# Soft-capped attention and a squared-ReLU MLP on one core: row sums and P times V on 32-column quarters, and scores as three float32r products from batch 1 on

## The chip, the core and the metric

One core of a Trainium2 chip runs the whole kernel. The metric is device time in microseconds (us) of one execution, as the median of several runs. Before the change it is 705.87 us (three runs, 705.72 to 706.65).

## What is computed

Two stages follow one another, both in float32:

```python
def _attn_ref(q, k, v, cap):                      # q, k, v: 4 x 12 x 448 x 64
    scale = 1.0 / np.sqrt(q.shape[-1])
    scores = scale * np.matmul(q, k.transpose(0, 1, 3, 2))
    scores = cap * np.tanh(scores / cap)
    scores = scores - np.max(scores, axis=-1, keepdims=True)
    attn = np.exp(scores)
    attn = attn / (np.sum(attn, axis=-1, keepdims=True) + 1e-09)
    return np.matmul(attn, v)
...
x = attn_out.transpose(0, 2, 1, 3).reshape(B * S, H * D)   # 1792 x 768
h = x @ w_in                                      # w_in 768 x 2048
r = np.maximum(h, 0.0)
return (r * r) @ w_out                            # w_out 2048 x 768
```

## The kernel before

**Attention** works on two heads at a time (`heads`, L158): a pair, six pairs for each of the four batches, 24 in all. q and k of a pair lie transposed in one tile `qkraw`, head 0 on partitions 0 to 63 and head 1 on 64 to 127. The 448 keys are cut into four chunks of 112. For each chunk TensorE (PE in the profile) makes the transposed scores of both heads (`qk`, L186): two float32 matmuls of 64 rows, which lie on different halves of the array's rows. ScalarE (ACT) takes the tanh (L195). VectorE (DVE) keeps a running maximum over the chunks (`top`, L203), GpSimd (POOL) reduces it over the partitions (`all_top`, L211), DVE subtracts it (`less`, through the helper `sub`, L143), ACT takes the exponential (L223). A tile `t` now holds unnormalised probabilities P of one chunk, keys on partitions, queries of head 0 and then head 1 along the row.

**P times V and the row sums.** `pv` (L249) multiplies each head's 64 columns of v by its half of `t`: head 0 to output partitions 0 to 63 of the PSUM tile `po`, head 1 to 64 to 127. `ones` (L261) does the same with 64 columns of ones instead of v, so that a second PSUM tile (`ss`, which shows as `po` too) holds the sum of each query on all 64 partitions of its head. Up to pair 10 that is done for each chunk; from pair `ADD_FROM` = 11 on DVE first adds the four chunks (`add`, L233, tile `ts`) and `ones` runs once for the pair. Then ACT copies the sums (`sums`, L282), DVE transposes them in blocks of 32 (`tr1`, L285), takes 14 reciprocals on each partition (`rec`, L288), spreads them back by a second transpose (`tr2`, L291), multiplies (`mult`, L296) and splits the result into a rounded high part (`x_hi`) and a rest (`x_lo`, L143): the tile `x`, two float32r halves.

**The MLP** runs batch by batch after that batch's attention: `up` makes 16 blocks of 128 hidden units, each over six `x` tiles; `down` makes six blocks of 128 outputs, each over 16 `g` tiles. Each pair of tiles costs three float32r matmuls of 128 x 128 x 448 (L389, L390, L391: low weight by high input, high by high, high by low). That is 576 matmuls for a batch; they show as `f<-x,w` and `f<-g,w` (in the last batch `ff`).

**Weights** come in as 34 pieces: 16 of w_in (one for each block of `up`), 18 of w_out. `convert` (L315) loads a piece into `raw`, unpacks it on DVE (L339, L342, L345), splits it into high and low halves (a copy on ACT or DVE, and L143), and stores the result to device memory; batch 0 uses it from where it was made, batches 1 to 3 load it back (L378).

**What sets the order.** Nothing is scheduled by hand line by line. Each piece of work is a `Step` with an engine, a due time (`key`), a duration and buffers. At build time a planner (L475 to L569) walks through them with an event queue: each engine takes the ready step with the smallest key whose buffers fit. What comes out is one fixed order for each engine; on the chip every engine runs its list in that order and waits where data is late. The constants of L38 to L47 set the keys: `C0` is the distance of the pairs of batch 0, `W` the length planned for each batch's MLP, `EARLY` how many weight pieces are converted while batch 0's attention still runs, `SPACE` the distance of the other pieces:

```python
t0 = 2.0 + i * (TF[0] - 10.0) / EARLY if i < EARLY else TF[0] + SPACE * (i - EARLY)
to[key] = convert(t0, src, dst, n)
```

## Time and profile before

| | |
|---|---|
| median of three runs | 705.87 us (705.72 to 706.65) |
| span of the profiled execution, first to last instruction | 704.5 us |
| PE busy in the span | 688.2 us (98%), 3300 matmul instructions |
| DVE busy | 423.2 us (60%) |
| ACT busy | 362.7 us (51%) |
| POOL busy | 86.5 us (12%) |
| DMA | 148.41 MB, 211 GB/s over the span |

The span is one execution, and it ends 1.37 us below the median of the runs. Matmul times overlap in the records: a matmul's bar begins before the bar of the one ahead of it has ended, so what a matmul costs in a stream is read from start to start, not from the length of its bar. A float32 matmul stands as two instructions in the trace and as one in the printed orders below. On the other engines, too, a bar is a little longer than the distance to the next start.

### The profile page before, as it was taken

What the parts mean: (1) busy time and instruction counts of PE and PEld (TensorE: products, weight loads), DVE (VectorE), ACT (ScalarE), POOL (GpSimd) and SP (SyncE); (2) the same over time, 40 slices, a digit from 0 to 9 for tenths busy, and PEclk for the clock granted to TensorE, in tenths of its full rate; (3) what the DMA queues carried; (4) which work ended last, traced back from release to release, by engine and by line L of the source; (5) the groups of instructions that cost most, each with busy time, mean ns of one, the idle gap of its engine ahead of it and who ended that gap; (6) DMA issues with size and microseconds to landing.
All of it is one profiled execution on the core that took longest, in us unless ns stands there. A gap on an engine that the chain in (4) does not pass through costs nothing.

```text
span 704.5 us, 8604 instructions
## 1 busy us (share of the span) xinstructions
PE 688.2 (98%) x3300; PEld 500.7 (71%) x3300; DVE 423.2 (60%) x563; ACT 362.7 (51%) x498; POOL 86.5 (12%) x28
## 2 busy tenths in 40 slices
PE   6799999999999999999999999999999999999997
PEld 2233367567876786776797866766679979999997
DVE  4999999999997984777630654887681011111000
ACT  5688686788565645757521444776661003443000
POOL 1532204202101021011100110111110000000000
PEclk9899999999999999999999999999999999999999
DMA  8813469897899879745466655743337666665760
GB/s 202 262 57 107 138 219 309 273 306 259 321 324 303 300 270 333 209 149 165 153 235 206 214 182 170 227 147 127 115 116 247 239 237 214 206 209 202 241 204 26
DMA packets 57304, 148.41 MB, mean 211 GB/s; under 512 B 26288, under 2 KB 35504, under 8 KB 57264
## 3 DMA queue, kind: packets, MB, share of 16 engines
q1 hardware_dynamic: 57264, 147.87, 64.1%
q8 instruction: 26, 0.43, 0.2%
q14 instruction: 14, 0.11, 0.0%
HBM read 117.18 MB, written 30.67 MB: 210 GB/s over the span
## 4 chain that ended last, share of the span: by engine, by line
PE 87%; DVE 7%; POOL 1%; issue 1%; DMA 1%; ACT 1%; SPq 0%; ACTq 0%; DVEq 0%
PE f L389 18%; PE f L391 17%; PE f L390 17%; PE po L249 8%; PE s L186 8%; PE ff L389 5%; PE ff L390 5%; PE ff L391 5%; PE po L261 4%; DVE t L143 3%; DVE mx L203 2%; POOL ma L211 1%; DMA raw<-in_w_in_dram 1%; ACT t L223 1%; DVE xf L296 1%
## 5 line engine op out<-in xcount | busy, mean ns | idle before, releaser
L211 POOL PARTITION_ALL_REDUCE ma<-mx x24 | 86.3, 3597 | 434.0 <-DVE mx L203 412.4
L223 ACT ACTIVATE t<-t,capa 112x896 f32<-112x896 f32 x96 | 99.0, 1040 | 39.4 <-DVE t L143 38.7
L389 PE MATMUL f<-x,w 128*128 128x448 f32 x300 | 114.6, 382 | 0.0
L391 PE MATMUL f<-x,w 128*128 128x448 f32 x300 | 109.7, 366 | 0.0
L390 PE MATMUL f<-x,w 128*128 128x448 f32 x300 | 109.6, 365 | 0.0
L143 DVE TENSOR_TENSOR t<-t,ma 112x896 f32<-112x896 f32 x96 | 105.1, 1109 | 4.3 <-POOL ma L211 3.6
L389 PE MATMUL f<-g,w 128*128 128x448 f32 x288 | 106.7, 371 | 0.0
L391 PE MATMUL f<-g,w 128*128 128x448 f32 x288 | 105.3, 366 | 0.0
L390 PE MATMUL f<-g,w 128*128 128x448 f32 x288 | 105.3, 366 | 0.0
L195 ACT ACTIVATE t<-s,c 112x896 f32<-112x896 f32 x96 | 93.1, 1000 | 18.6 <-PE s L186 18.4
L186 PE MATMUL s<-qkraw 64*112 64x448 f32 x384 | 88.5, 575 | 6.4 <-DMA qkraw<-in_qkT_dram 4.7
L143 DVE TENSOR_TENSOR g<-r,g 128x448 fp32r<-128x448 f32 x64 | 40.4, 632 | 84.7 <-ACT g L138 84.6
L249 PE MATMUL po<-t,v 112*64 112x448 f32 x384 | 84.7, 553 | 4.7 <-ACT t L223 4.6
L389 PEld LDWEIGHTS f<-x,w 128*128 128x128 f32 x300 | 56.3, 188 | 35.1 <-issue 26.6
L186 PEld LDWEIGHTS s<-qkraw 64*112 64x112 f32 x384 | 31.7, 178 | 47.5 <-issue 29.8
L389 PEld LDWEIGHTS f<-g,w 128*128 128x128 f32 x288 | 54.1, 188 | 13.1 <-issue 8.9
L391 PEld LDWEIGHTS f<-x,w 128*128 128x128 f32 x300 | 56.4, 188 | 4.6
L249 PEld LDWEIGHTS po<-t,v 112*64 112x64 f32 x384 | 24.3, 137 | 49.7 <-issue 37.4
L390 PEld LDWEIGHTS f<-x,w 128*128 128x128 f32 x300 | 56.5, 188 | 3.8
L285 DVE STREAM_TRANSPOSE tr<-sm 128x448 f32<-128x448 f32 x24 | 15.4, 640 | 71.1 <-ACT sm L282 71.0
L391 PEld LDWEIGHTS f<-g,w 128*128 128x128 f32 x288 | 54.1, 188 | 4.3
L390 PEld LDWEIGHTS f<-g,w 128*128 128x128 f32 x288 | 54.2, 188 | 4.1
(52 smaller groups left out, 855.8 us busy)
## 6 DMA issues: line engine op xcount, KB each, us to landing
w<-k_in SPq DMA_DIRECT2D x48, 768.0 KB, 4.8
w<-k_out SPq DMA_DIRECT2D x36, 640.0 KB, 3.9
w<-k_out SPq DMA_DIRECT2D x18, 768.0 KB, 4.6
raw<-in_w_in_dram SPq DMA_DIRECT2D x16, 768.0 KB, 7.3
k_in<-w SPq DMA_DIRECT2D x16, 768.0 KB, 4.4
qkraw<-in_qkT_dram SPq DMA_DIRECT2D x48, 224.0 KB, 5.6
raw<-in_w_out_dram SPq DMA_DIRECT2D x12, 640.0 KB, 5.7
k_out<-w SPq DMA_DIRECT2D x12, 640.0 KB, 3.7
```

Of the source, the lines that this page charges most:

```text
L143: nc.vector.tensor_tensor(out=out, in0=in0, in1=in1, op=ALU.subtract)
L186: nc.tensor.matmul(s[c].ap[0:CP, i, 0:S], raw.ap[r, 1, ks], raw.ap[r, 0], start=True, stop=True)
L195: nc.scalar.activation(out=t[c].ap, in_=s[c].ap[0:CP, :, 0:S], func=AF.Tanh, scale=c1[0:CP])
L203: nc.vector.tensor_tensor(out=mx.ap, in0=t[0].ap if c == 1 else mx.ap, in1=t[c].ap, op=ALU.max)
L211: nc.gpsimd.partition_all_reduce(ma.ap, mx.ap, CP, RED.max)
L223: nc.scalar.activation(out=t[c].ap, in_=t[c].ap, func=AF.Exp, scale=capa[0:CP])
L249: nc.tensor.matmul(po.ap[rows[i], 0:S], vs[i].ap[:, c, rows[i]], t[c].ap[:, i], start=c == 0, stop=c == NCH - 1)
L261: nc.tensor.matmul(ss.ap[rows[i], 0:S], vs[i].ap[:, 0, rows[1 - i]], u.ap[:, i], start=start, stop=stop)
L285: nc.vector.transpose(out=tr.ap, in_=sm.ap)
L389: nc.tensor.matmul(o, w.ap[:, 1, j], x[:, 0], start=first and j == 0, stop=False)
L390: nc.tensor.matmul(o, w.ap[:, 0, j], x[:, 0], start=False, stop=False)
L391: nc.tensor.matmul(o, w.ap[:, 0, j], x[:, 1], start=False, stop=last and j == n - 1)
```

## The change

Four things change together.

1. `pv` and `ones` use quarters: four matmuls of 32 columns in place of two of 64. A quarter of `pv` is one half of a head's v columns over all 448 queries; a quarter of `ones` is one head's ones over half of the queries (224), so the tile of sums is 224 wide. `sums` and `tr1` get half as long, `rec` becomes four instructions. The rows of `x` come out in another order (32 by 32), and w_in's rows are loaded in that order, by four transfers of 32 partitions for a piece in place of one of 128.
2. From pair `SPLIT_FROM` = 6 on (batch 1 and later) q and k are split into a rounded part (`qkhi`, a copy on ACT or DVE) and a rest (`qklo`, a subtraction on DVE), and a chunk's scores are three float32r products for each head in place of one float32 product.
3. `ADD_FROM` goes from 11 to 12.
4. The planner's constants and the durations it uses for the changed steps are new; among them `EARLY` goes from 1 to 4.

```diff
@@ -32,19 +32,21 @@
     CP, NCH = v.shape[1], v.shape[3]
     NM, P, NKK, _ = w_in.shape
     NDM, _, NF, _ = w_out.shape
+    Q, SH = D // 2, S // 2
     WP = [(0, 6), (6, 5), (11, 5)]
     SCALE = 1.0 / float(D) ** 0.5
     REBASE = 2.0**-112
-    EARLY, SPACE = 1, 3.4
-    ATT, WLEAD = -6, 14
-    NBLK, NHLF, NW, XB, NT = 37, 13, 7, 10, 10
-    C0, LAT, TAIL = 4, 28, 30
-    DMA, QSTEP, HOLD, PORT = 2.5, 2, 4, 15
-    PVD, QD = 6, 2
-    XH, GH, WH = 0.0, -2.0, 0.0
-    ADD_FROM = 11
+    EARLY, SPACE = 4, 2.4
+    ATT, WLEAD = -4, 13
+    NBLK, NHLF, NW, XB, NT = 37, 13, 7, 10, 12
+    C0, LAT, TAIL = 5.0, 27, 32
+    DMA, QSTEP, HOLD, PORT = 2.5, 2, 5.0, 15.0
+    PVD, QD = 8, 2
+    XH, GH, WH = 5, -1, 4
+    ADD_FROM, SPLIT_FROM = 12, 6
+    SPLIT_DUE, NSPLIT, SPARE_H, SPARE_L, SPARE_Q = 2, 1, 2, 2, 4
     PSTEP = [2, 2, 4, 4]
-    W = [140, 145, 150, 120]
+    W = [135, 160, 160, 120]
 
     const = ctx.enter_context(tc.tile_pool(name="const", bufs=1))
     sb = ctx.enter_context(tc.tile_pool(name="sb", bufs=2))
@@ -83,7 +85,8 @@
 
     SIZES = {"blk": NBLK, "hlf": NHLF, "w": NW, "s": 2, "acc": 4, "rc": 2, "free": 1 << 20}
     TAGS = {
-        "qkraw": ("blk", [P, 2, S], F32, 3, 5),
+        "qkraw": ("blk", [P, 2, S], F32, 3, SPARE_Q),
+        "qkhi": ("blk", [P, 2, S], F32R, NSPLIT, SPARE_H), "qklo": ("blk", [P, 2, S], F32R, NSPLIT, SPARE_L),
         "s": ("s", [P, 2, 512], F32, 2, 0), "po": ("acc", [P, 512], F32, 4, 0), "f": ("acc", [P, 512], F32, 2, 0), "ff": ("acc", [P, 512], F32, 4, 0),
         "t": ("blk", [CP, 2, S], F32, NT, 2), "ts": ("blk", [CP, 2, S], F32, 2, 1),
         "mx": ("blk", [CP, 2, S], F32, 2, 2), "ma": ("blk", [CP, 2, S], F32, 2, 1),
@@ -173,6 +176,20 @@
                 nc.sync.dma_start(out=vs[i].ap[:, :, i * D:(i + 1) * D], in_=v[b, :, h + i])
 
         ready = Step(T - 16, "SP", 1.5, load, new=[raw], lag=3.0)
+        n_split = p >= SPLIT_FROM
+        operands = [raw]
+        if n_split:
+            hi, lo = Buf("qkhi"), Buf("qklo")
+            operands = [hi, lo]
+
+            def qk_hi(eng):
+                copy(eng, hi.ap, raw.ap)
+
+            def qk_lo():
+                sub(lo.ap, raw.ap, f(hi.ap))
+
+            a = Step(T - SPLIT_DUE, None, COPY(896), qk_hi, [ready], new=[hi], use=[raw])
+            ready = Step(T - SPLIT_DUE + 0.5, "DVE", SUB(896), qk_lo, [a], new=[lo], use=[raw, hi], port=True)
         got_v = Step(T, "SP", 1.4, load_v, new=vs, lag=3.0)
 
         tanhs = []
@@ -181,14 +198,17 @@
             def qk(c0=c0):
                 for c in range(c0, c0 + n_at):
                     ks = slice(c * CP, (c + 1) * CP)
-                    for i in range(2):
-                        r = slice(i * D, (i + 1) * D)
-                        nc.tensor.matmul(
-                            s[c].ap[0:CP, i, 0:S], raw.ap[r, 1, ks], raw.ap[r, 0], start=True, stop=True
-                        )
+                    pairs = [(lo, hi), (hi, hi), (hi, lo)] if n_split else [(raw, raw)]
+                    for n, (kk, qq) in enumerate(pairs):
+                        for i in range(2):
+                            r = slice(i * D, (i + 1) * D)
+                            nc.tensor.matmul(
+                                s[c].ap[0:CP, i, 0:S], kk.ap[r, 1, ks], qq.ap[r, 0],
+                                start=n == 0, stop=n == len(pairs) - 1,
+                            )
 
             cs = slice(c0, c0 + n_at)
-            q = Step(T + (2 if b == 0 else QD) * c0, "PE", 0.75 * n_at, qk, [ready], new=s[cs] + t[cs], use=[raw], mode="rows")
+            q = Step(T + (2 if b == 0 else QD) * c0, "PE", (0.57 if n_split else 0.75) * n_at, qk, [ready], new=s[cs] + t[cs], use=operands, mode="rows")
             for c in range(c0, c0 + n_at):
 
                 def tanh(c=c):
@@ -240,14 +260,16 @@
                 ]
 
 
-        rows = [slice(0, D), slice(D, 2 * D)]
+
+        quarters = [(i, a, slice((2 * a + i) * Q, (2 * a + i + 1) * Q)) for a in range(2) for i in range(2)]
 
         def pv(c0, n):
             def go():
                 for c in range(c0, c0 + n):
-                    for i in range(2):
+                    for i, a, to in quarters:
+                        d0 = i * D + a * Q
                         nc.tensor.matmul(
-                            po.ap[rows[i], 0:S], vs[i].ap[:, c, rows[i]], t[c].ap[:, i], start=c == 0, stop=c == NCH - 1
+                            po.ap[to, 0:S], vs[i].ap[:, c, d0:d0 + Q], t[c].ap[:, i], start=c == 0, stop=c == NCH - 1
                         )
                     if not n_add:
                         ones(t[c], c == 0, c == NCH - 1)
@@ -257,9 +279,11 @@
             return go
 
         def ones(u, start, stop):
-            for i in range(2):
+
+            for i, a, to in quarters:
+                d0 = (1 - i) * D
                 nc.tensor.matmul(
-                    ss.ap[rows[i], 0:S], vs[i].ap[:, 0, rows[1 - i]], u.ap[:, i], start=start, stop=stop
+                    ss.ap[to, 0:SH], vs[i].ap[:, 0, d0:d0 + Q], u.ap[:, i, a * SH:(a + 1) * SH], start=start, stop=stop
                 )
 
         n_pv = PSTEP[b]
@@ -269,7 +293,7 @@
             end = c1_ == NCH
             pvs.append(
                 Step(
-                    T + 17 + 2 * (c1_ - 1) + (PVD if b else 0), "PE", (0.75 if n_add else 1.5) * n_pv + (0.75 if n_add and end else 0),
+                    T + 17 + 2 * (c1_ - 1) + (PVD if b else 0), "PE", (0.75 if n_add else 1.125) * n_pv + (0.375 if n_add and end else 0),
                     pv(c0, n_pv), exps[c0:c1_] + [got_v] + pvs[-1:] + adds * end,
                     new=[po, ss] if c0 == 0 else [],
                     use=t[c0:c1_] + vs + ([po, ss] if c0 else []) + ([ts] if n_add and end else []), mode="cols",
@@ -279,13 +303,18 @@
         sm, tr, rc, xf, x = Buf("sm"), Buf("tr"), Buf("rc"), Buf("xf"), Buf("x")
 
         def sums():
-            nc.scalar.activation(out=sm.ap, in_=ss.ap[:, 0:S], func=AF.Identity, bias=eps)
+            nc.scalar.activation(out=sm.ap[:, 0:SH], in_=ss.ap[:, 0:SH], func=AF.Identity, bias=eps)
 
         def tr1():
-            nc.vector.transpose(out=tr.ap, in_=sm.ap)
+            nc.vector.transpose(out=tr.ap[:, 0:SH], in_=sm.ap[:, 0:SH])
 
         def rec():
-            nc.vector.reciprocal(out=rc.ap, in_=tr.ap.rearrange("p (j c) -> p j c", c=32)[:, :, 0])
+            for a in range(2):
+                own = tr.ap[a * D:(a + 1) * D, 0:SH].rearrange("p (j c) -> p j c", c=32)[:, :, 0]
+                for to in range(2):
+                    nc.vector.reciprocal(
+                        out=rc.ap[to * D:(to + 1) * D, a * SH // 32:(a + 1) * SH // 32], in_=own
+                    )
 
         def tr2():
             nc.vector.transpose(
@@ -302,9 +331,9 @@
             sub(x.ap[:, 1], xf.ap, f(x.ap)[:, 0])
 
         T += 26
-        a = Step(T, "ACT", 0.63, sums, pvs[-1:], new=[sm], use=[ss])
-        a = Step(T + 1, "DVE", 0.57, tr1, [a], new=[tr], use=[sm])
-        a = Step(T + 1, "DVE", 0.17, rec, [a], new=[rc], use=[tr])
+        a = Step(T, "ACT", 0.42, sums, pvs[-1:], new=[sm], use=[ss])
+        a = Step(T + 1, "DVE", 0.33, tr1, [a], new=[tr], use=[sm])
+        a = Step(T + 1, "DVE", 0.6, rec, [a], new=[rc], use=[tr])
         a = Step(T + 1, "DVE", 0.56, tr2, [a], use=[rc, sm])
         a = Step(T + 1, "DVE", 0.54, mult, [a] + pvs[-1:], new=[xf], use=[sm, po])
         a = Step(T + 2, None, COPY(448, dve=XH), x_hi, [a], new=[x], use=[xf])
@@ -312,13 +341,19 @@
         x_t[b, h // 2], xdone[b, h // 2] = x, a
 
 
-    def convert(T, src, dst, n):
+    def convert(T, src, dst, n, by_quarters):
         raw, u, mag, w = Buf("raw", [P, n * P]), Buf("u", [P, n * P]), Buf("mag", [P, n * P]), Buf("w", [P, 2, n, P])
         flat = lambda: u.ap.bitcast(F32)
         part = lambda i: w.ap[:, i].rearrange("p n c -> p (n c)")
 
         def load():
-            nc.sync.dma_start(out=raw.ap, in_=src.rearrange("p n c -> p (n c)"))
+            if not by_quarters:
+                nc.sync.dma_start(out=raw.ap, in_=src.rearrange("p n c -> p (n c)"))
+                return
+            rows = src.rearrange("(i a r) n c -> i a r (n c)", i=2, a=2)
+            for i in range(2):
+                for a in range(2):
+                    nc.sync.dma_start(out=raw.ap[(2 * a + i) * Q:(2 * a + i + 1) * Q], in_=rows[i, a])
 
         def word(i):
             return raw.ap.bitcast(U32).rearrange("p (n t) -> p n t", t=2)[:, :, i]
@@ -459,7 +494,7 @@
     ]
     for i, (to, key, src, dst, n) in enumerate(pieces):
         t0 = 2.0 + i * (TF[0] - 10.0) / EARLY if i < EARLY else TF[0] + SPACE * (i - EARLY)
-        to[key] = convert(t0, src, dst, n)
+        to[key] = convert(t0, src, dst, n, to is conv_in)
     for b in range(B):
         t0, rate = TF[b], W[b] / (NM * NKK + NDM * NF)
         for m in range(NM):
```

**Where the order moves.** VectorE, between the end of the fifth and of the sixth `x` tile (the last of batch 0; `x<-xf,x` is `x_lo`). Before:

```order
L143 TENSOR_TENSOR x<-xf,x 128x448
L342 TENSOR_SCALAR u<-raw 128x768
L285 STREAM_TRANSPOSE tr<-sm 128x448
L143 TENSOR_TENSOR t<-t,ma 112x896
L288 RECIPROCAL rc<-tr 128x14
L143 TENSOR_TENSOR t<-t,ma 112x896
L291 STREAM_TRANSPOSE sm<-rc 128x448
L345 SCALAR_TENSOR_TENSOR u<-mag,u 128x768
L296 TENSOR_TENSOR xf<-po,sm 128x448
L140 CAST w<-u 128x768
L143 TENSOR_TENSOR t<-t,ma 112x896
L143 TENSOR_TENSOR x<-xf,x 128x448
```

In the change:

```order
L374 TENSOR_SCALAR u<-raw 128x768
L146 TENSOR_TENSOR qklo<-qkraw,qkhi 128x896
L377 TENSOR_SCALAR u<-raw 128x768
L380 SCALAR_TENSOR_TENSOR u<-mag,u 128x768
L309 STREAM_TRANSPOSE tr<-sm 128x224
L315 RECIPROCAL rc<-tr 64x7 x4
L146 TENSOR_TENSOR t<-t,ma 112x896
L320 STREAM_TRANSPOSE sm<-rc 128x448
L146 TENSOR_TENSOR w<-u,w 128x768
L325 TENSOR_TENSOR xf<-po,sm 128x448
L146 TENSOR_TENSOR t<-t,ma 112x896
L146 TENSOR_TENSOR x<-xf,x 128x448
```

A whole weight piece (both L374/L377 halves, L380 and the `w` subtraction) and a `qklo` subtraction stand ahead of that tile now, the transposed sums are 224 wide, and the reciprocal is four instructions. Over the whole list up to the sixth `x` tile, six weight pieces are done in the change, and three before (with a fourth unpacked), and two `qklo` subtractions are new.

TensorE, the last chunk of the fourth pair and what follows it. `v_2` and `v_3` are the tiles that hold v and the ones of the two heads. Before:

```order
L249 MATMUL po<-t,v_2_110 64x448
L249 MATMUL po<-t,v_3_112 64x448
L261 MATMUL po<-t,v_2_110 64x448
L261 MATMUL po<-t,v_3_112 64x448
L389 MATMUL f<-x,w 128x448
L390 MATMUL f<-x,w 128x448
L391 MATMUL f<-x,w 128x448
L186 MATMUL s<-qkraw 112x448 x4
```

In the change:

```order
L271 MATMUL po<-t,v_2_110 32x448
L271 MATMUL po<-t,v_3_112 32x448
L271 MATMUL po<-t,v_2_110 32x448
L271 MATMUL po<-t,v_3_112 32x448
L285 MATMUL po<-t,v_2_110 32x224
L285 MATMUL po<-t,v_3_112 32x224
L285 MATMUL po<-t,v_2_110 32x224
L285 MATMUL po<-t,v_3_112 32x224
L205 MATMUL s<-qkhi,qklo 112x448 x2
L205 MATMUL s<-qkhi 112x448 x2
L205 MATMUL s<-qklo,qkhi 112x448 x2
```

A chunk has eight quarters where it had four halves, the ones' quarters 224 wide; the float32 scores (`qkraw`, two chunks in the one row before) have become three float32r products for a chunk.

SyncE, which issues the transfers, where the conversion of w_in is under way. Before:

```order
L321 DMA raw<-in_w_in_dram 128x768
L356 DMA k_in_69<-w 128x1536
L321 DMA raw<-in_w_in_dram 128x768 x2
L356 DMA k_in_70<-w 128x1536
L356 DMA k_in_71<-w 128x1536
L321 DMA raw<-in_w_in_dram 128x768
L173 DMA v_0_106<-in_v_dram 112x4x64
L173 DMA v_1_108<-in_v_dram 112x4x64
L356 DMA k_in_72<-w 128x1536
L321 DMA raw<-in_w_in_dram 128x768
```

In the change:

```order
L356 DMA raw<-in_w_in_dram 32x768 x4
L172 DMA qkraw<-in_qkT_dram 64x2x448 x2
L356 DMA raw<-in_w_in_dram 32x768 x8
L391 DMA k_in_72<-w 128x1536
L176 DMA v_0_106<-in_v_dram 112x4x64
L176 DMA v_1_108<-in_v_dram 112x4x64
L356 DMA raw<-in_w_in_dram 32x768 x8
L391 DMA k_in_73<-w 128x1536
L391 DMA k_in_74<-w 128x1536
L356 DMA raw<-in_w_in_dram 32x768 x8
```

Each piece of w_in is four rows' worth of issues, and two pieces are asked for together.

## Rows read from the trace of the kernel before

**Rows 1.** The page, busy tenths of DVE in 40 slices of the span.

```profile
DVE  4999999999997984777630654887681011111000
```

**Rows 2.** Windows: length, busy us (instructions) of PE, PEld, DVE, ACT, POOL; clock, DMA share, GB/s.

```profile
0.00:93.78 93.78, 81.03 (x359) 29.62 (x359) 84.08 (x105) 67.94 (x78) 28.42 (x11) 0.96 0.52 145
93.78:259.98 166.20, 166.20 (x801) 118.94 (x800) 158.77 (x226) 113.61 (x158) 24.89 (x6) 1.00 0.88 302
259.98:704.50 444.52, 440.94 (x2145) 352.18 (x2143) 180.32 (x234) 181.16 (x264) 33.21 (x11) 1.00 0.58 191
```

**Rows 3.** Timeline of PE, four places: start, us, engine, line, matmul.

```profile
93.78 0.47 PE L389 MATMUL f<-x,w 128*128 128x448 f32 x1
...
259.98 0.36 PE L389 MATMUL f<-x,w 128*128 128x448 f32 x1
...
584.03 0.36 PE L389 MATMUL f<-g,w 128*128 128x448 f32 x1
...
700.56 0.36 PE L391 MATMUL ff<-g,w 128*128 128x448 f32 x1
```

**Rows 4.** Timeline of PE, a step of scores, and one of P times V.

```profile
95.19 1.76 PE L186 MATMUL s<-qkraw 64*112 64x448 f32 x8
...
104.07 0.37 PE L391 MATMUL f<-x,w 128*128 128x448 f32 x1
104.37 0.97 PE L249 MATMUL po<-t,v 112*64 112x448 f32 x4
...
107.84 0.36 PE L390 MATMUL f<-x,w 128*128 128x448 f32 x1
```

**Rows 5.** Timeline of weight loads in the same P times V step.

```profile
104.37 0.20 PEld L249 LDWEIGHTS po<-t,v 112*64 112x64 f32 x4 [0.31 <-issue]
104.80 0.14 PEld L261 LDWEIGHTS po<-t,v 112*64 112x64 f32 x2 [0.23 <-issue]
```

**Rows 6.** The page, groups of weight loads: busy us and mean ns of one.

```profile
L186 PEld LDWEIGHTS s<-qkraw 64*112 64x112 f32 x384 | 31.7, 178 | 47.5 <-issue 29.8
...
L249 PEld LDWEIGHTS po<-t,v 112*64 112x64 f32 x384 | 24.3, 137 | 49.7 <-issue 37.4
```

**Rows 7.** Timeline of DVE around the sixth x tile.

```profile
86.71 0.62 DVE L285 STREAM_TRANSPOSE tr<-sm 128x448 f32<-128x448 f32 x1
...
88.23 0.22 DVE L288 RECIPROCAL rc<-tr 128x14 f32<-128x14 f32 x1
88.37 1.02 DVE L143 TENSOR_TENSOR t<-t,ma 112x896 f32<-112x896 f32 x1
...
89.87 0.91 DVE L345 SCALAR_TENSOR_TENSOR u<-mag,u 128x768 uint32<-128x768 uint32 x1
90.71 0.61 DVE L296 TENSOR_TENSOR xf<-po,sm 128x448 f32<-128x448 f32 x1
91.24 0.54 DVE L140 CAST w<-u 128x768 fp32r<-128x768 f32 x1
91.70 1.08 DVE L143 TENSOR_TENSOR t<-t,ma 112x896 f32<-112x896 f32 x1
92.71 0.61 DVE L143 TENSOR_TENSOR x<-xf,x 128x448 fp32r<-128x448 f32 x1
93.24 0.95 DVE L143 TENSOR_TENSOR w<-u,w 128x768 fp32r<-128x768 f32 x1
94.11 1.08 DVE L143 TENSOR_TENSOR t<-t,ma 112x896 f32<-112x896 f32 x1
95.11 1.08 DVE L339 TENSOR_SCALAR u<-raw 128x768 uint16<-128x768 uint16 x2
```

**Rows 8.** Tile raw: landing; timelines of SP and DVE: a load's issue, its first use.

```profile
DMA to landing us min/median/max: 4.9/6.3/10.3
...
110.34 0.42 SPq L321 DMA_DIRECT2D raw<-in_w_in_dram  x1
...
120.55 0.62 DVE L339 TENSOR_SCALAR u<-raw 128x768 uint16<-128x768 uint16 x1
```

## The prediction

> **What bounds the kernel now.** I read the slices of the page first, then the windows, then the timelines of PE and DVE. The slices show DVE full from the second slice to the thirteenth, 18 to 229 us [rows 1], and far from it behind that, so the 60% of the table is an average over very different stages. The windows put the first border at 93.78 us: before it PE is busy for 81 of 94 us, with overlapping bars, behind it without a gap [rows 2]. That is the start of the first MLP matmul that reads the sixth `x` tile [rows 3], which DVE finishes just before: its last part starts at 92.71 [rows 7]. From there on PE has no gap: 166.20 busy of 166.20 us up to 259.98, where the first matmul of batch 1's MLP stands, and all of the rest but the tail [rows 2, 3]. DVE is still busy for 158.77 of those 166.20 us (96%), and for 180.32 of the last 444.52 [rows 2]. So there are three stages: up to 93.78 DVE, with PE waiting; up to 259.98 PE, with DVE close behind; then PE alone. PE's clock is 1.00, its upper level of 2.4 GHz, in the last two.
>
> **Prices on PE, start to start.** The 576 matmuls of the last MLP have nothing among them: 584.03 to 700.56 is 575 intervals [rows 3], 0.2027 us each. A step of two chunks of P times V with ones (8 float32 rounds, two heads side by side) lies between two MLP matmuls at 104.07 and 107.84 [rows 4]: 3.77 us. I take a float32 round of 448 columns as 0.75 us for a chunk's pair, so 3.00 for the step; less two MLP matmuls (0.41) that leaves 0.36 for going in and out of the mode, 0.18 a change; I use 0.19. A score step of two chunks has a bar of 1.76 [rows 4], which agrees with 0.75 a chunk.
>
> These prices must give the time before. In the order before, from 93.78 on, stand 2274 MLP matmuls (460.9), 66 score chunks (49.5), 70 chunks of P times V (52.5), 31 of ones (23.25) and 109 changes of mode (20.7): 606.9 us. 93.78 + 606.9 = 700.7, and the last matmul starts at 700.56 and takes 0.20. The sum closes, so nothing else is on PE's path.
>
> **PE's part of the change.** In the new order the same point (the first MLP matmul that reads the sixth `x` tile, the 31st in both) is followed by 2274 MLP matmuls, 64 score chunks, all as three products, 72 chunks of P times V, 36 of ones, 105 changes.
> - Ones: a quarter has half the columns, so 0.375 a chunk if four quarters run side by side as two halves do: 36 x 0.375 = 13.5 in place of 23.25, though there are more of them (one pair fewer is added on DVE).
> - P times V: quarters of 448 columns, 0.75 a chunk as before if four run side by side: 54.0.
> - Scores: three rounds of one float32r product, two heads side by side. The trace has no such product on 64 rows; the nearest is the 128-row one at 0.2027. I take 0.608 a chunk: 38.9. The lower bound is the float32 price over four passes, 0.1875 a round (0.56 a chunk, 2.9 less in all), the upper 0.75 a chunk (9 more).
> - Changes: 20.0.
>
> With 460.9 that is 587.3, or 19.6 less than 606.9.
>
> Two prices above rest on four quarters side by side, which the trace of before does not show. What it shows is two halves side by side: four weight loads begin within 0.06 us of each other (0.20 for four bars of 0.137), and the next two begin at 104.80, while matmuls run [rows 5, 6]. A load takes 178 ns for 112 columns and 137 for 64 [rows 6], so I estimate 0.11 for 32. Four of them, 0.02 apart, take 0.17 a round: hidden under a round of 0.375, and only just under the ones' round of 0.19. The lower bound for a chunk of ones is 0.375, the upper 0.75 (no gain).
>
> The Trainium skill speaks against this, in "TensorE: Matmul & The Clock Gate", Part 3: loads of weights overlap running matmuls only where the row group differs, and quarters that share their 112 rows do not differ in it. Here the trace disagrees: the two halves share their rows too, and the loads at 104.80 begin beside running matmuls. By that rule each quarter round would show its 0.17 us of loads, and the sum would be that of the third rival below.
>
> **DVE's part, up to the sixth x tile.** PE starts its gapless run when DVE has made that tile, so every microsecond that DVE's list grows ahead of it moves the run. Counted in the two orders up to there, priced start to start [rows 7]: four more unpacking halves (0.50 each, 2.0), two more L380 (0.84, 1.7), three more `w` subtractions (0.87, 2.6), two `w` copies fewer (0.46, -0.9), two `qklo` subtractions (priced as a `t` one, 1.01: 2.0) and one `t` subtraction fewer (-1.0); six transposes of half the width (0.62 now; I estimate 0.25 off each, -1.5); 24 reciprocals in place of six (0.14 each, 2.5). Sum: **7.4 us**. The small reciprocals are the unknown: between a quarter of 0.14 each, as a quarter of the work (5 in place of 7.4), and the whole bar of 0.22 (9.3). I stay with 0.14: a transpose of 448 columns has a bar of 0.62, so little of a 14-column instruction's 0.14 can go with its length.
>
> So the tile's last part starts at 92.71 + 7.4 = 100.1, ends 0.53 later, and PE's run starts near 100.8 in place of 93.78. PE has less to do before (ones and scores are cheaper there too) and simply waits more: what the change saves in this stage buys nothing.
>
> **After that, up to the end of batch 0's MLP.** PE: 546 MLP matmuls (110.7), 20 score chunks (12.2), 24 of P times V (18.0), 24 of ones (9.0), 42 changes (8.0): 157.9 in place of 166.2. That puts the start of batch 1's MLP at 258.7, against 259.98 now. DVE has 158.77 us in this stage now; the pieces done earlier leave it, and five more `qklo` and a `qkhi` copy come in: to the last weight piece the two lists add up alike (within 1 us), so it has some 152 us in 158. It stays just ahead. What hides it is thin, and I come back to it. The work on ACT (some `qkhi` copies at about 1 us, shorter `sums`) lies in a stage with 113.61 busy of 166.20 [rows 2].
>
> Then PE alone: 587.3 - 157.9 = 429.4 in place of 606.9 - 166.2 = 440.7, so 11.3 us less. The other eleven `qklo`, the `qkhi` copies and the small reciprocals on DVE, some 25 us, lie in 444 us of which it uses 180: hidden.
>
> **w_in in four transfers.** An issue holds SP for about 0.4 us [rows 8], so the last quarter of a piece is asked for 1.2 us later. A load lands 6.3 us after its issue (median), and the piece asked for at 110.34 is first touched at 120.55 [rows 8], so 4 us are spare: nothing, if four transfers of 32 partitions together move like one of 128. If they went one after the other, each as long as the whole, it would be 25 us a piece.
>
> **Sum.** 100.8 + 587.3 = 688.1 for the last matmul; the tail to the end of the span is 704.5 - 700.8 = 3.7; span 691.8. The median of the runs lies 1.4 above the profiled span: **693.2 us**, 12.7 faster. Own range 686 to 700: scores -2.9 to +3 (half way to the upper bound), reciprocals -2.4 to +2, ones up to +4.5 if a round takes a quarter longer than its columns.
>
> **Rivals.**
> 1. Quarters run two at a time. Then a round of four costs double: after the start of the run 54.0 + 13.5 = 67.5 us more, 761. For it: no row shows more than two side by side. Against: the loads of the next round stand beside the present one without loss. This is the one that ends slower, and it decides early: the gain of 12.7 is gone once quarter rounds take 19% longer than I price them.
> 2. DVE or the loads fall behind between 100 and 259. The lists are nearly equal there (DVE 96% busy [rows 2]), DMA is at 0.88, and a quartered load that lands 4 us late holds DVE, then PE, one for one. Price 5 to 15 us: 698 to 708.
> 3. The quarters' loads are not hidden: 216 rounds x 0.17 = 37 us, 730. If only the ones' short rounds suffer, up to no gain from them: 13.5, 707. For it: 0.17 under 0.19 is close. Against: loads beside running matmuls [rows 5].
> 4. DVE's additions ahead of the sixth tile cost nothing, because it now waits in places that they fill: 686. Against: the slices show no such holes [rows 1].
>
> **Chances.** Forecast 0.58, rival 1 0.06, rival 2 0.13, rival 3 0.13 (0.05 in full, 0.08 for ones only), rival 4 0.10. A measurement tells 0.2%, 1.4 us, from no change. Faster: forecast, rival 4, most of rival 2: 0.79. Same: 0.06, from the ones-only case and the end of rival 2. Slower: 0.15. The range 684 to 707 leaves out rivals 1 and 3 in full, a little of rival 2, and the best of rival 4: about 0.18.
>
> **What would show it.** Right: PE's gapless run starts at 99 to 102 and the 577th MLP matmul at 257 to 261; eight quarters of P times V and eight of ones take 2 x 1.125 us for two chunks; scores 1.2 us for two chunks. Wrong: steps of P times V that are longer than before, gaps of PE between 100 and 259 that end with `w` or `raw`, or a run that starts as early as before.

## The result, and the profile after

The changed kernel takes **697.44 us** (median of four runs, 696.38 to 698.09), beside 705.88 us (705.72 to 706.65) for the kernel before on the same chip: a ratio of 0.9874, with an interval of 0.9861 to 0.9888. The forecast was 693.2 us, with a range of 684 to 707. The profiled execution took 698.09 us, its span is 696.3.

**The three stages** stand in the windows (length, busy us of PE, PEld, DVE, ACT, POOL; clock, DMA share, GB/s) and in the timeline of PE at their borders; they answer to [rows 2] and [rows 3]. L424 to L426 are now the lines of the MLP matmuls, L205 the scores, L271 P times V, L285 the ones, L146 the helper `sub`.

```profile
0.00:101.29 101.29, 73.26 (x559) 29.04 (x559) 91.72 (x129) 71.28 (x83) 29.96 (x11) 0.93 0.58 156
101.29:262.09 160.80, 160.73 (x1050) 123.05 (x1051) 154.82 (x233) 114.04 (x162) 30.95 (x6) 0.98 0.91 292
262.09:696.30 434.21, 430.30 (x2473) 357.90 (x2471) 206.23 (x298) 181.21 (x264) 33.87 (x11) 1.00 0.63 197
```

```profile
98.16 0.45 PE L205 MATMUL s<-qkhi,qklo 64*112 64x448 f32 x2 [1.22 <-ACT t L215]
...
101.29 0.74 PE L424 MATMUL f<-x,w 128*128 128x448 f32 x1 [2.27 <-ACT x L141]
...
262.09 0.37 PE L424 MATMUL f<-x,w 128*128 128x448 f32 x1
...
692.02 0.37 PE L426 MATMUL ff<-g,w 128*128 128x448 f32 x1
```

PE's gapless run starts at 101.29 in place of 93.78 and batch 1's MLP at 262.09 in place of 259.98. The change is 2.1 us late there, and makes all of its gain in the stage in which PE is alone: from 262.09 to the end of the last matmul are 430.1 us, against 440.8. The middle stage has no gap, but its clock is 0.98.

**What released the run** differs between the two kernels. Before, PE's last wait was for `xf` (the product that the sixth tile is made from) at 91.37; from there to 93.78 it worked through P times V and ones, and the first matmul on the sixth tile waited for nothing. In the change nothing stands in between: DVE makes `xf`, ACT rounds it, and PE starts. Timelines of PE before, then of DVE and ACT in the change:

```profile
91.37 0.97 PE L261 MATMUL po<-t,v 112*64 112x448 f32 x4 [0.52 <-DVE xf L296]
```

```profile
99.95 0.61 DVE L325 TENSOR_TENSOR xf<-po,sm 128x448 f32<-128x448 f32 x1
100.66 0.58 ACT L141 ACTIVATE x<-xf 128x448 fp32r<-128x448 f32 x1 [0.94 <-DVE xf L325]
```

**The quarters** run four side by side. Two chunks of P times V and ones between two MLP matmuls, in PE's timeline:

```profile
114.96 0.37 PE L426 MATMUL f<-x,w 128*128 128x448 f32 x1
115.26 0.96 PE L271 MATMUL po<-t,v 112*32 112x448 f32 x8
116.03 0.56 PE L285 MATMUL po<-t,v 112*32 112x224 f32 x8
116.41 0.94 PE L271 MATMUL po<-t,v 112*32 112x448 f32 x8
117.16 0.56 PE L285 MATMUL po<-t,v 112*32 112x224 f32 x8
117.66 0.47 PE L424 MATMUL f<-x,w 128*128 128x448 f32 x1
117.97 0.36 PE L425 MATMUL f<-x,w 128*128 128x448 f32 x1
```

From 114.96 to 117.97 are 3.01 us: two MLP matmuls (0.41), two changes of mode (from 128-row matmuls to quarters and back), and the quarters. With 0.18 for a change, as before, the quarters take 2.25, which is 2 x (0.75 + 0.375). The timeline of weight loads answers to [rows 5]:

```profile
115.26 0.16 PEld L271 LDWEIGHTS po<-t,v 112*32 112x32 f32 x8 [0.31 <-issue]
115.66 0.13 PEld L285 LDWEIGHTS po<-t,v 112*32 112x32 f32 x4 [0.25 <-issue]
```

Eight loads with a mean of 112 ns (the page's group) lie in one bar of 0.16, and the next four begin at 115.66, while the matmuls of 115.26 run. The Trainium skill, in "TensorE: Matmul & The Clock Gate", Part 3, lists that loads overlap running matmuls only where the row group differs, while its text above the list also excepts loads to the background weight buffer. By the list alone a load's time would stand between the rounds; the trace disagrees, as it did for the halves. Which buffer a load goes to, no run here shows.

**The scores** of two chunks, PE's timeline again:

```profile
147.05 0.37 PE L426 MATMUL f<-x,w 128*128 128x448 f32 x1
147.34 0.46 PE L205 MATMUL s<-qkhi,qklo 64*112 64x448 f32 x2
147.64 0.37 PE L205 MATMUL s<-qkhi 64*112 64x448 f32 x2
...
149.05 0.37 PE L425 MATMUL f<-x,w 128*128 128x448 f32 x1
```

147.05 to 149.05 is 2.00 us: 0.41 for two MLP matmuls, 0.38 for two changes, and 1.21 for six rounds, 0.202 each and 0.606 a chunk, as priced (0.608).

**DVE ahead of the sixth `x` tile**, its timeline beside [rows 7]:

```profile
94.06 2.28 DVE L380 SCALAR_TENSOR_TENSOR u<-mag,u 128x768 uint32<-128x768 uint32 x1
96.26 0.40 DVE L309 STREAM_TRANSPOSE tr<-sm 128x224 f32<-128x224 f32 x1
96.69 0.82 DVE L315 RECIPROCAL rc<-tr 64x7 f32<-64x7 f32 x4
97.55 1.09 DVE L146 TENSOR_TENSOR t<-t,ma 112x896 f32<-112x896 f32 x1
...
101.48 0.62 DVE L146 TENSOR_TENSOR x<-xf,x 128x448 fp32r<-128x448 f32 x1
```

Four reciprocals of 64x7 take 0.86 from start to start, 0.21 each, and not 0.14. The tile's last part starts at 101.48, forecast 100.1. L380 takes 2.28 here, and about 0.9 elsewhere; the last section comes back to that.

**The clock** in windows of 2 us around the start of the run (same columns as above; the last three numbers begin with the clock):

```profile
96.00:98.00 2.00, 0.94 (x7) 0.45 (x6) 1.90 (x7) 1.63 (x2) 0.71 (x1) 1.00 0.00 0
98.00:100.00 2.00, 0.85 (x6) 0.45 (x6) 2.00 (x4) 1.16 (x2) 0.00 (x0) 1.00 0.00 0
100.00:102.00 2.00, 0.71 (x2) 0.50 (x2) 2.00 (x4) 1.34 (x2) 0.00 (x0) 0.51 0.63 246
102.00:104.00 2.00, 2.00 (x10) 1.22 (x12) 2.00 (x3) 2.00 (x4) 0.00 (x0) 0.50 0.93 234
...
106.00:108.00 2.00, 2.00 (x25) 0.68 (x17) 2.00 (x3) 2.00 (x5) 0.00 (x0) 0.78 0.99 215
108.00:110.00 2.00, 2.00 (x11) 1.86 (x11) 2.00 (x4) 0.89 (x2) 0.36 (x1) 1.00 1.12 256
```

PE is busy for under half of 96 to 102, with waits of 1.22 and 2.27 us for ACT, and then starts its run at 1.2 GHz. From 101.29 to 106 at half the clock it loses 2.35 us of work, from 106 to 108 at 0.78 another 0.44: 2.8 in all. The forecast for this stage was 157.9 us, and it took 160.80. The size of the loss differs from one execution to the next: a second profile of the same kernel (the run "changed kernel once more" below) has the stage from 101.36 to 260.83, 159.47 us.

### The profile page after: what moved, and what is told of

Its sections match the earlier page's. It is cut to its first block, busy times and chain, and to the rows that moved or that the text cites. A ratio compares the mean times of both kernels' runs of the same rounds, so it can differ in the third digit from the quotient of the medians.

```text
span 696.3 us, 10384 instructions
## 1 busy us (share of the span) xinstructions
PE 664.3 (95%) x4080; PEld 510.0 (73%) x4080; DVE 452.8 (65%) x658; ACT 366.5 (53%) x508; POOL 94.8 (14%) x28
## 4 chain that ended last, share of the span: by engine, by line
PE 86%; DVE 9%; issue 2%; DMA 1%; ACT 1%; SPq 1%; DVEq 0%; ACTq 0%
PE f L424 18%; PE f L426 17%; PE f L425 17%; PE po L271 8%; PE s L205 8%; PE ff L426 5%; PE ff L424 5%; PE ff L425 5%; DVE t L146 3%; PE po L285 2%; DVE mx L223 1%; DVE u L380 1%; DMA raw<-in_w_in_dram 1%; DVE w L146 1%; DVE rc L315 1%
## 5 line engine op out<-in xcount | busy, mean ns | idle before, releaser
L231 POOL PARTITION_ALL_REDUCE ma<-mx x24 | 94.6, 3945 | 452.2 <-DVE mx L223 360.8
L424 PE MATMUL f<-x,w 128*128 128x448 f32 x300 | 114.9, 383 | 2.9 <-ACT x L141 2.3
L426 PE MATMUL f<-x,w 128*128 128x448 f32 x300 | 110.6, 369 | 1.0 <-DVE x L146 0.9
L146 DVE TENSOR_TENSOR t<-t,ma 112x896 f32<-112x896 f32 x96 | 107.2, 1132 | 5.0 <-POOL ma L231 4.6
L424 PE MATMUL f<-g,w 128*128 128x448 f32 x288 | 107.0, 371 | 0.0
L426 PE MATMUL f<-g,w 128*128 128x448 f32 x288 | 105.3, 365 | 0.0
L271 PE MATMUL po<-t,v 112*32 112x448 f32 x768 | 87.3, 561 | 8.6 <-ACT t L243 7.9
L223 DVE TENSOR_TENSOR mx<-mx,t 112x896 f32<-112x896 f32 x48 | 51.9, 1082 | 58.0 <-ACT t L215 57.2
L146 DVE TENSOR_TENSOR g<-r,g 128x448 fp32r<-128x448 f32 x64 | 40.9, 643 | 72.7 <-ACT g L141 72.5
L424 PEld LDWEIGHTS f<-x,w 128*128 128x128 f32 x300 | 56.6, 189 | 22.3 <-issue 11.8
L426 PEld LDWEIGHTS f<-x,w 128*128 128x128 f32 x300 | 56.6, 189 | 7.3 <-DVE x L146 2.5
L424 PEld LDWEIGHTS f<-g,w 128*128 128x128 f32 x288 | 54.1, 188 | 9.7 <-issue 5.1
L426 PEld LDWEIGHTS f<-g,w 128*128 128x128 f32 x288 | 54.1, 188 | 4.4
L271 PEld LDWEIGHTS po<-t,v 112*32 112x32 f32 x768 | 21.6, 112 | 43.5 <-issue 27.8
L442 ACT ACTIVATE r<-f 128x448 f32<-128x448 f32 x50 | 27.0, 542 | 43.3 <-PE f L426 42.9
L471 ACT ACTIVATE o<-f 128x448 f32<-128x448 f32 x18 | 9.7, 542 | 73.6 <-PE f L426 73.6
```

Source lines behind the costliest of these rows:

```text
L146: nc.vector.tensor_tensor(out=out, in0=in0, in1=in1, op=ALU.subtract)
L223: nc.vector.tensor_tensor(out=mx.ap, in0=t[0].ap if c == 1 else mx.ap, in1=t[c].ap, op=ALU.max)
L231: nc.gpsimd.partition_all_reduce(ma.ap, mx.ap, CP, RED.max)
L271: nc.tensor.matmul(po.ap[to, 0:S], vs[i].ap[:, c, d0:d0 + Q], t[c].ap[:, i], start=c == 0, stop=c == NCH - 1)
L424: nc.tensor.matmul(o, w.ap[:, 1, j], x[:, 0], start=first and j == 0, stop=False)
L426: nc.tensor.matmul(o, w.ap[:, 0, j], x[:, 1], start=False, stop=last and j == n - 1)
```

## The experiments

Two theories stood against each other for the 4.2 us by which the forecast was too low: that PE's clock fell around the long wait (**the clock**), and that DVE or the loads were slightly late in the middle stage (**lateness**). Beside them, several prices of the forecast were put to a run. Times stand as medians and as ratios to the kernel before in the same series (706.27 to 706.66 us).

**Halves instead of quarters.** The order of the work is kept; P times V and the ones go back to halves, the reciprocals to one instruction, a `w_in` piece to one transfer.

```diff
-                    for i, a, to in quarters:
+                    for i in range(2):
...
-            nc.vector.transpose(out=tr.ap[:, 0:SH], in_=sm.ap[:, 0:SH])
+            nc.vector.transpose(out=tr.ap, in_=sm.ap)
...
+            nc.vector.reciprocal(out=rc.ap, in_=tr.ap.rearrange("p (j c) -> p j c", c=32)[:, :, 0])
...
-            if not by_quarters:
+            if True:
```

> The changed kernel in its own order on every engine, but P times V and the row sums on 64-column halves again (sums 448 wide, one reciprocal, w_in in one transfer). My theory: behind the first MLP matmul that reads the sixth x tile stand 36 chunks of ones, 0.375 us dearer each: +13.5. Ahead of it DVE has 18 reciprocals fewer (24 x 0.20 against 6 x 0.14: -4.0) and six wider transposes (+1.5), so the run starts 2.5 earlier; the loss by the slower clock behind the wait (2.8) may go with it. 697.4 + 13.5 - 2.5 = 708.4, or 705.6 if the clock stays up. Rival, that the new order and not the quarters brings the gain: 697 to 698.

It took 713.32 us, ratio 1.0100 (1.0083 to 1.0116): slower than the kernel before, where 705.6 to 708.4 was expected. From the start of batch 1's MLP on, the ones cost what they should: 262.09 to 692.02 is 429.93 in the changed kernel, 271.29 to 705.75 is 434.46 here, and the 4.5 more are 12 x 0.375. The rest was lost earlier. Its last matmul, and two of its windows:

```profile
705.75 0.37 PE L420 MATMUL ff<-g,w 128*128 128x448 f32 x1
```

```profile
0.00:102.89 102.89, 82.59 (x366) 30.54 (x366) 88.56 (x111) 72.06 (x83) 29.47 (x11) 0.93 0.55 153
102.89:271.29 168.40, 167.26 (x858) 123.53 (x859) 150.71 (x216) 114.12 (x163) 27.38 (x6) 1.00 0.82 281
```

DVE has 18 instructions fewer ahead of the run, and still the run starts at 102.89, 1.6 us later. The view of DVE's waits up to there (total us, times, longest) says why:

```profile
DVE x L146 <- ACT x L141: 3.0, 2, 2.3
DVE tr L308 <- ACT sm L305: 2.4, 3, 1.0
```

Neither row is there for the changed kernel up to 101, where the waits of DVE on work of other engines are 6.5 us at the start and then one of 0.2. PE's longer steps of ones (82.59 us busy against 73.26) make the scores and the sums late; ACT waits for them (2.05 us for scores at 53.85, for one), and DVE behind it. PE's saving ahead of the run was not idle after all.

**One float32 product of the rounded parts.** The splitting stays, but scores are one float32 product: their rests are left out.

```diff
-                    pairs = [(lo, hi), (hi, hi), (hi, lo)] if n_split else [(raw, raw)]
+                    pairs = [(hi, hi)] if n_split else [(raw, raw)]
...
-                                s[c].ap[0:CP, i, 0:S], kk.ap[r, 1, ks], qq.ap[r, 0],
+                                s[c].ap[0:CP, i, 0:S], f(kk.ap)[r, 1, ks], f(qq.ap)[r, 0],
```

`f(...)` hands the rounded part over as float32.

> The changed kernel in its own order, the split of q and k still done on DVE and ACT, but each chunk's scores as one float32 product of the rounded parts (the rests are left out of the scores). My theory: 64 chunks on PE's gapless path at 0.75 in place of 0.608: +9.1, so 706.5; the eight chunks ahead of the run are hidden. Rival, that the three products save nothing where they stand: 697.4.

706.21 us, ratio 0.9997 (0.9988 to 1.0006), as expected. From the start of batch 1's MLP to the last matmul it takes 435.94 us, 6.0 more than the changed kernel; the 44 chunks there at 0.142 each give 6.2.

```profile
263.77 0.36 PE L424 MATMUL f<-x,w 128*128 128x448 f32 x1
...
699.71 0.37 PE L426 MATMUL ff<-g,w 128*128 128x448 f32 x1
```

**Twelve MLP matmuls moved into the hole.** Four sets of three, on `x` tiles 4 and 5 of the first two units, go to just ahead of the first matmuls on the sixth tile.

```diff
...
+            prev[0].place = (b, m, j)
...
+    late = [st for st in ISSUE if getattr(st, "place", None) in [(0, 0, 3), (0, 0, 4), (0, 1, 3), (0, 1, 4)]]
+    ISSUE[:] = [st for st in ISSUE if st not in late]
+    at = next(i for i, st in enumerate(ISSUE) if getattr(st, "place", None) == (0, 0, 5))
+    ISSUE[at:at] = late
```

> The changed kernel with four groups of MLP matmuls (12 matmuls, hidden units 0 and 1 by x tiles four and five) moved on PE from earlier to right before the first matmul that reads the sixth x tile, where PE waits 2.27 us; all other engines keep their order. My theory, that the clock fell to 0.5 behind that wait and cost 2.8 us of the stretch to batch 1: granted clock 1.00 from 100 us on, the run starts at 101.3 to 101.8, batch 1's first MLP matmul at 259 to 260, time 694.8. Rival, that the stretch is longer because weights or DVE are late: 697.4, the same 262 for batch 1.

696.62 us, ratio 0.9859 (0.9845 to 0.9874), 1.8 above what was expected. Taking the matmuls from where they stood left a hole there: PE is busy for 1.82 of 94 to 98, and the clock is 0.63 from 98 to 102. The clock had been expected at 1.00 from 100 us on; it fell earlier, and is back at 1.00 from 102. So the run starts at 102.18, but the stage behind it takes 157.82 us (102.18 to 260.00).

**The same matmuls redone.** Nothing moves; ahead of the sixth tile the first unit's 15 matmuls on tiles 1 to 5 run once more into the same sums, started anew.

```diff
+                if again and j == 5:
+                    for jj in range(5):
+                        x = rhs[jj].ap
+                        nc.tensor.matmul(o, w.ap[:, 1, jj], x[:, 0], start=jj == 0, stop=False)
+                        nc.tensor.matmul(o, w.ap[:, 0, jj], x[:, 0], start=False, stop=False)
+                        nc.tensor.matmul(o, w.ap[:, 0, jj], x[:, 1], start=False, stop=False)
...
```

> The changed kernel, but before the first MLP matmul that reads the sixth x tile PE computes hidden unit 0's first five products once more (15 matmuls, 3.0 us of work that brings nothing, in the 2.27 us wait). By the clock theory: the run starts 0.8 later and the clock stays at 1.00, so 697.4 + 0.8 - 2.8 = 695.4, faster although there is more to do. Rival, that the clock isn't what it lost: 697.4 + 0.8 = 698.2.

695.93 us, ratio 0.9849 (0.9835 to 0.9864), which overlaps with the interval of the changed kernel; what counts here is the trace. The windows of 98 to 102 and of the stage, and its one wait in PE's timeline:

```profile
98.00:102.00 4.00, 4.00 (x21) 3.61 (x20) 4.00 (x6) 3.06 (x4) 0.00 (x0) 1.00 0.56 172
...
101.25:260.42 159.17, 157.67 (x1051) 122.06 (x1050) 152.19 (x232) 112.98 (x161) 27.32 (x6) 1.00 0.92 294
```

```profile
184.35 0.47 PE L431 MATMUL f<-g,w 128*128 128x448 f32 x1 [1.50 <-DVE w L146]
```

With PE kept busy the clock stays at 1.00 and the stage's work takes 157.67 us. But now DVE is late once, by 1.50 us: lateness appears when the loss by the clock is gone.

**One transfer per `w_in` piece.** The host hands `w_in` over with its rows in the new order.

```diff
-            if not by_quarters:
+            if True:
...
-        "w_in": moe_w_in.view(np.int64).reshape(DM // P, P, DFF // P, P).transpose(2, 1, 0, 3),
+        "w_in": moe_w_in.view(np.int64).reshape(DM // P, 2, 2, 32, DFF // P, P).transpose(0, 2, 1, 3, 4, 5).reshape(DM // P, P, DFF // P, P).transpose(2, 1, 0, 3),
```

> The changed kernel in its own order, but w_in's rows are laid out in the order of the quarters in device memory beforehand, so that a piece of w_in is one transfer of 128 partitions again (16 issues in place of 64). My theory, that four transfers cost nothing: the same within a measurement, 697.4 (696.4 to 698.4), the same 160.8 us from the start of the run to batch 1. Rival, that late quarters of w_in hold DVE in the first 150 us: up to 3 us less, and the start of the run earlier.

698.24 us, ratio 0.9892 (0.9875 to 0.9908), the stage from 101.55 to 261.15: nothing is gained. The page lists the issues of w_in's pieces with their size and the median us from issue to landing, with four transfers and then with one:

```profile
raw<-in_w_in_dram SPq DMA_DIRECT2D x64, 192.0 KB, 5.3
```

```profile
raw<-in_w_in_dram SPq DMA_DIRECT2D x16, 768.0 KB, 6.2
```

A quarter lands 5.3 us after its own issue, the whole piece 6.2 after its. So the four quarters move side by side; the 25 us of the prediction's "one after the other" do not arise.

**A weight piece later.** The unpacking of the sixth piece (six steps with its store) moves behind the sixth `x` tile on every engine.

```diff
...
+        made.append(steps[-6:])
...
+    late = [st for st in ISSUE if st in made[5]]
+    last_x = xdone[0, H // 2 - 1]
+    early = [st for st in late if ISSUE.index(st) < ISSUE.index(last_x)]
+    ISSUE[:] = [st for st in ISSUE if st not in early]
+    at = ISSUE.index(last_x) + 1
+    ISSUE[at:at] = early
```

> The changed kernel with the unpacking of the sixth weight piece (two halves, the whole, its copy, its rest and its store; 2.8 us of DVE) moved from before to right after the last part of the sixth x tile; PE keeps its order. My theory, that each microsecond of DVE's list ahead of that tile moves the start of PE's run: the start at 98.3 to 99.3 in place of 101.3, no wait for x, clock 1.00 behind it. But DVE's list up to the last piece stays as long, so PE runs into waits for w of 1 to 2 us between 100 and 200, and batch 1 starts at 258.5 to 260: 694 to 695.5, the gain being mostly the clock's. Rival, that something else (PE, ACT) sets the start: 101, and 697.4.

697.86 us, ratio 0.9882 (0.9867 to 0.9896): nothing gained, against 694 to 695.5. PE's timeline:

```profile
98.91 0.47 PE L427 MATMUL f<-x,w 128*128 128x448 f32 x1 [1.23 <-ACT x L141]
...
104.47 0.58 PE L272 MATMUL po<-t,v 112*32 112x448 f32 x4 [0.76 <-ACT t L244]
...
127.51 0.47 PE L427 MATMUL f<-x,w 128*128 128x448 f32 x1 [1.72 <-DVE w L146]
```

The run starts 2.4 us earlier, as it should, and batch 1 at 262.06, where it stood (262.09). Two things were expected otherwise: a wait of 1.23 for `x` is left ahead of the run, and the clock is 0.91 from 100 to 120, not 1.00. The stage takes 163.15 us in place of 160.80: 2.48 are the two waits in it. What is taken from DVE's list ahead of the run is owed right behind it.

**The new code under the old planner's constants**, `ADD_FROM` = 11 among them.

```diff
-    EARLY, SPACE = 4, 2.4
-    ATT, WLEAD = -4, 13
+    EARLY, SPACE = 1, 3.4
+    ATT, WLEAD = -6, 14
...
-    XH, GH, WH = 5, -1, 4
-    ADD_FROM, SPLIT_FROM = 12, 6
+    XH, GH, WH = 0.0, -2.0, 0.0
+    ADD_FROM, SPLIT_FROM = 11, 6
...
-    W = [135, 160, 160, 120]
+    W = [140, 145, 150, 120]
```

> All of the change's code (quarters, four transfers, split scores), but the planner's constants of the kernel before (and its due times and lead values), which gives another order on every engine. Adding up its lists at the same prices: the sixth x tile 3.6 us later than in the change, batch 1 about 6 us later, the end 4.5 later. My theory: 699 to 703. Rival, that the gain is the retuned order's: 705 or more; rival, that the constants do nothing: 697.

715.54 us, ratio **1.0131** (1.0112 to 1.0149): slower than before, far off the 699 to 703. PE's timeline, and two windows:

```profile
67.89 0.60 PE L285 MATMUL po<-t,v 112*32 112x224 f32 x4 [5.04 <-DVE xf L325]
...
85.17 0.60 PE L285 MATMUL po<-t,v 112*32 112x224 f32 x4 [5.19 <-DVE xf L325]
...
108.79 0.60 PE L285 MATMUL po<-t,v 112*32 112x224 f32 x4 [3.06 <-DVE xf L325]
```

```profile
80.00:100.00 20.00, 13.32 (x117) 5.80 (x121) 17.44 (x28) 8.86 (x11) 3.49 (x2) 0.83 0.36 114
100.00:120.00 20.00, 16.27 (x115) 10.03 (x107) 12.83 (x21) 11.04 (x15) 2.17 (x1) 0.83 0.43 114
```

PE waits for DVE's `xf`, which frees its PSUM tile, and DVE itself is idle for 2.6 and 7.2 us of these windows. The first matmul on the sixth tile starts at 111.94, 10.7 us later than in the changed kernel, where 3.6 was expected. Engines that wait for one another in turn are in no sum of lists. All of the loss lies ahead of batch 1's MLP: from its first matmul (279.15) to the last one (710.19) are 431.0 us, nearly the 429.9 of the changed kernel. So the cheaper matmuls give the gain behind batch 1 in either order, and the order decides whether it is lost ahead of it. The rival of the expectation, that the gain is the new order's, has its time (705 or more), but the order by itself is not enough: with halves in the new order the kernel is slower than before.

**Three more in one series.** The changed kernel once more; all `w_hi` copies on ACT, to take load off DVE; and that together with the redone matmuls.

```diff
+    for st in ISSUE:
+        if st.fn.__name__ == "w_hi":
+            st.eng = "ACT"
```

> The changed kernel unaltered, as the measure of the two runs beside it: 0.987 of the time before, 697 us, the start of PE's run at 101 to 102, the clock at 0.83 to 0.91 in the stretch from 100 to 120.

> The changed kernel with all copies of the weights' rounded half on ACT (the seven that DVE does go to ACT, none of them ahead of the sixth x tile), nothing else moved. It takes 2.3 us off DVE's list between the sixth x tile and the twentieth weight piece. My theory: the start (101.3) and the fall of the clock stay, no wait for w was there to remove: 696.4 to 697.4. Rival, that DVE's list sets the time of the whole stretch to batch 1: 2 to 3 less, 695.

> Both: the 15 repeated matmuls that keep PE at work through the wait for the sixth x tile, and the weight copies on ACT. My theory: the clock stays at 1.00 behind the start (worth 2.8), and the 1.5 us wait for w that the first of these met at 184 us is gone, so batch 1 starts at 258.5 to 259.5 and the time is 694 to 694.8, the best of all. Rival, that another wait takes its place: 695.6, as with the repeat alone.

In that order: 696.34 us, ratio 0.9863 (0.9849 to 0.9877); 697.48, 0.9870 (0.9856 to 0.9883); 695.84, 0.9850 (0.9837 to 0.9864). The changed kernel came out as expected (start at 101.36, clock 0.91 from 100 to 120). The copies alone change nothing that can be told from it, though the run starts at 102.36 and not, as expected, at 101.3. Both together give the stage as it was forecast, in the windows:

```profile
101.69:259.37 157.68, 157.68 (x1051) 122.19 (x1050) 149.33 (x224) 117.64 (x168) 32.10 (x6) 1.00 0.92 297
```

No wait, clock 1.00, 157.68 us. It has the shortest median of the series, but its interval overlaps with that of the changed kernel: it cannot be called faster than that one.

## Why the prediction was right, and where not

The forecast held in kind and in size (12.7 us faster, 8.4 measured), by its own mechanism: a later start of the run, paid back by cheaper work on PE.

- **Prices on PE: right.** Ones at 0.375, P times V at 0.75, scores at 0.608 a chunk and 0.19 a change give 429.4 us from the start of batch 1's MLP on; 430.1 were measured. The runs with halves (4.5 us for 12 chunks) and with one float32 product (6.0 for 44) confirm two of them singly.
- **DVE's list ahead of the sixth tile: 7.4 us, 8.8 measured** (92.71 to 101.48). The mis-sized term is the reciprocals: 24 times 0.07 more than 0.14 is 1.7. Summed start to start over both timelines of DVE, the reciprocals grow by 4.1 (forecast 2.5) and all else by 4.7 (forecast 4.9); in the latter, single terms are off by up to 1.9, both ways, since other instructions are the slow ones beside GpSimd (last section).
- **The start of the run: 100.8, and 101.29 measured, in part by luck.** The prediction lets the run follow the tile's last part by 0.7 us. But before, the first matmul on the tile waited for no part of it (91.37, above); in the change it waits for the rounded part from ACT, and starts 0.2 ahead of the last part. `xf` moved by 9.2 us, the run by 7.5. The list was 1.4 too short and the distance 0.9 too long, and that leaves 0.5.
- **The stage up to batch 1: 157.9, and 160.80 measured.** This is the mis-sized term that counts. The step that failed is that PE "simply waits more" ahead of the run, as if that had no price behind it: with PE waiting, the clock fell to 1.2 GHz, and the run began with 2.8 us lost (1.8 in the second profile, 159.47 less 157.67). That the clock is the cause is shown by three runs: where PE was kept busy (157.67 of work, and 157.68) and where the clock had fallen and risen earlier (157.82) the stage took what was forecast. In the changed kernel itself lateness has nothing to explain: the stage has 0.07 us of gaps.
- **"What the change saves in this stage buys nothing": wrong.** With halves the run starts 1.6 us later although DVE's list is shorter. I estimate what the cheaper ones ahead of the run were worth at some 4 us: the 1.6, and the 2.5 by which the start was expected earlier.
- **Counting lists: a lower bound that the new order happens to reach.** The prediction gave the new constants no term of their own. The same code under the old constants takes about 18 us more (715.54 against 697.44). The prediction came near the time because DVE's list in the new order is nearly free of waits; the prediction did not work that out, so it is luck too. The constants were changed together, so which of them matter is not shown.
- **Four transfers at nothing: right**, by the run with one.
- **The own range of 686 to 700** does not follow from its terms. A quarter more for the 36 chunks of ones is 3.4, not 4.5, and the terms then add up to 688 to 702. The page has DVE full up to the twelfth slice; the thirteenth stands at 7 [rows 1]. Neither changes the forecast.
- **Rivals.** One (two quarters at a time) and three (loads not hidden) fall with the timelines at 115. Four falls: DVE's list did move the run. Two is the live one: no wait in the changed kernel, but 1.50 and 1.72 us for `w` as soon as the run went faster or sooner.

Of the 4.2 us, 2.9 are the stage up to batch 1. The rest: 0.5 at the start, 0.7 behind batch 1, 0.4 in the tail (4.1 for 3.7), less 0.3 since the median lies 1.1 above the span and not 1.4.

## What to carry to other kernels

Price matmuls start to start from the nearest rows and make the prices give the old time first; here that was good to 0.7 us in 430. Where two engines are nearly level, a sum over one's list is only a lower bound, and what one edit takes off it is owed at the next place: look for the engine that is second, and for the order that keeps both fed. A wait ahead of a dense stretch can cost more than its length, since the stretch may begin at the lower clock: here 1.8 and 2.8 us more.

## What was not expected of the hardware

- PE's clock fell from 2.4 to 1.2 GHz around two short waits, of 1.22 and 2.27 us: PE was busy for 0.94, 0.85 and 0.71 of 2 us in the windows ahead of the fall and at it. The clock was back at 1.00 in the window from 108.
- A reciprocal of 64x7 costs 0.21 us start to start, one of 128x14, with four times the elements, 0.14 [rows 7].
- The same DVE instruction (L380) took 2.28 us at 94.06 where its like at 89.87 of the kernel before took 0.91 [rows 7]. It lies within one of GpSimd's reductions over the partitions, and the kernel before has the same at another place (the half piece L339, else about 0.6):

```profile
92.17 4.54 POOL L231 PARTITION_ALL_REDUCE ma<-mx  x1 [13.94 <-DVE mx L223]
```

```profile
83.08 3.27 POOL L211 PARTITION_ALL_REDUCE ma<-mx  x1 [10.73 <-DVE mx L203]
83.38 1.85 DVE L339 TENSOR_SCALAR u<-raw 128x768 uint16<-128x768 uint16 x1
```

Up to the sixth tile, each of the seven such reductions in either trace has beside it at least one DVE instruction that is 0.5 to 1.5 us longer than its like, 8.7 us in all before and 8.5 in the change: a cost of both kernels, and not of the change. That the reduction is the cause was not tried.
